# The end of an attention and gated-layer decode step: the result over 128 partitions, one 16-byte-run store, three rows of wo in eight-column products

## The chip, the cores and the metric

The kernel runs on one core of one Trainium2 chip. The metric is the device time of one launch in microseconds (us), of which the runs before the change gave 228.76 to 228.85, median 228.85. All times below are of this core. A core has a matrix engine (TensorE, in the profile PE, with its weight loads under PEld), VectorE (DVE), ScalarE (ACT), GpSimd (POOL), and SyncE (SP), which issues nearly all of this kernel's DMA. Products are summed in PSUM, everything else on the chip lies in SBUF, and both have 128 partitions.

## The reference, cut to what is computed

```python
x = A_x                                  # [2, 1, 512], two batches
xn = layernorm(x)
q = (xn @ wq) -> 32 heads of 128         # wq [512, 4096]
k, v = the last 4096 keys of the caches  # 8 key heads, each used by 4 query heads
o = softmax(q k^T / sqrt(128)) v         # [2, 32*128]
gate, up = xn @ W_gate, xn @ W_up        # [512, 1792]
h = gate * (gate > 0) * up
return x + o @ wo + h @ W_down           # wo [4096, 512], W_down [1792, 512]
```

Everything is f32. The output is two rows of 512 numbers, 4 KB; the inputs that are read are about 95 MB.

## The kernel before, in words

The inputs come in pieces of up to 4 MB through a ring of four SBUF buffers, all issued on SyncE's queue in the order of the program: `wq` in two pieces, `W_gate`, `W_up`, then for each of four groups of heads two pieces of `k` and two of `v`, then `W_down` (tile `dw`, in the profile `wd`), then `wo`. A piece is issued when its ring buffer has been read for the last time. The two halves of `x` come on ScalarE's queue.

Keys are transposed by VectorE (L257) and multiplied with the queries (L262); softmax, the products with the values (L325), a mask (L334) and a gather (L345) follow. The last group's results are spread over partitions in `spread_heads` (L363): TensorE makes tile `op`, and ScalarE copies it to `oT` (two columns a row of `wo`, one for each batch) and the last rows' part to `oT_rows`.

The end of the program is what the change is about. `o @ wo + h @ W_down + x` is a sum over 14 rows `k` of `W_down` and over 32 rows of `wo` (16 of `wo0`, 16 of `wo1`, index j), where a "row" holds 512 output columns for each of 128 partitions. There are two ways of adding one row:

- *Wide* (`project_wide`, L425): one product, two result rows (the batches) by 512 columns, into `yw_ps`. The n-th wide product goes to the strip of partitions that begins at 32 x (n mod 4), so that four strips of the array work at a time, each with partial sums of its own. ScalarE then copies `yw_ps` to `yw` (L459), and the *fold*, a product with a matrix of zeros and ones (`fold_rows`), adds the four strips.
- *Narrow* (`project`, L431): the 512 columns are cut in four quarters of 128, and each quarter's product goes to another strip of `y_ps`. The stationary operand has 17 columns, of which the first and the last are the batches and the rest zeros, so that the batches come to partitions 32e and 32e + 16. The fold and `x` go the same way.

Before the change 14 + 16 + 8 rows go wide and the last eight rows of `wo1` (`LAST`) go narrow. The first four of these come before the fold, j=12 to 14 and then j=15 (in two halves) after it. VectorE copies `y_ps` to `yo` (L467), and the store (L469) takes the 8 partitions that hold something, 2 runs of 64 numbers from each. `wo1` is loaded in pieces of 4, 4, 4, 2 and 1 rows (L448) and the last row in two halves (L454).

The order of the program is the order of each engine's queue (there is no scheduler). An instruction that waits holds up what stands behind it on its engine.

Of the kernel before, what the change touches and what calls it, by code (L numbers as in the profile page):

```python
# [9 lines left out]
F32 = mybir.dt.float32  # L10
# [10 lines left out]
def kernel(  # L21
# [12 lines left out]
    nc = tc.nc  # L34
    P = 128
    B, _, D = x.shape
# [5 lines left out]
    KC = D // P  # L42
# [3 lines left out]
    Q = 4  # L46
    C = 4
    R = HKV // C
# [6 lines left out]
    FB = F // P  # L55
# [19 lines left out]
    def load_wq(m):  # L75
        src = wq.rearrange("(p k) f -> p k f", p=P)[:, 2 * m:2 * m + 2, :]
        return load(f"wq{m}", src, [P, 2, HQ * DH])
# [17 lines left out]
    NJ = HQ * DH // (R * P)  # L95
# [3 lines left out]
    def wo_rows(r, j0, j1):  # L99
        rows = NJ * P  # L100
        return wo[r * rows:(r + 1) * rows, :].rearrange("(p j) e -> p j e", p=P)[:, j0:j1, :]


    x2 = const.tile([B, D], F32, name="x2")
    for half in (slice(0, D // 2), slice(D // 2, D)):
        nc.scalar.dma_start(x2[:, half], x[:, 0, half])
    wqt = [load_wq(m) for m in range(2)]

    ident = const.tile([P, P], F32, name="ident")
# [24 lines left out]
        out=pick[:, 8:16], in_=ident.rearrange("p (q u k) -> p k q u", q=Q, u=4), op=ALU.add, axis=AX.XY  # L134
# [3 lines left out]
        out=own_u, in_=ident.rearrange("p (q u k) -> p u q k", q=Q, u=4), op=ALU.add, axis=AX.XY  # L138
    )
    fold = const.tile([P, 32], F32, name="fold")  # L140
    nc.vector.tensor_reduce(
        out=fold, in_=ident.rearrange("p (q i) -> p i q", q=Q), op=ALU.add, axis=AX.X
    )
    fold_rows = const.tile([P, B, 16], F32, name="fold_rows")
    nc.gpsimd.memset(fold_rows, 0.0)
    nc.gpsimd.tensor_copy(fold_rows[:, :, 0], fold[:, 0:B])
    LAST = 8
    oT_rows = const.tile([P, LAST, B, 16], F32, name="oT_rows")
    nc.gpsimd.memset(oT_rows, 0.0)

    def rows(t):
        return t.rearrange("p b s -> p (b s)")[:, 0:17]


    HK = 2 * REP
# [2 lines left out]
    for h in range(2):  # L158
        nc.vector.tensor_reduce(
            out=by_h[:, :, h], in_=ident[:, PK * h:PK * h + PK].rearrange("p (x t k) -> p t k x", t=NP, k=REP),  # L160
            op=ALU.add, axis=AX.X,
# [29 lines left out]
        )  # L191
    xnT = const.tile([P, KC, 32], F32, name="xnT")
    nc.vector.tensor_copy(xnT, xt_ps)
    spare = const.tile([P, KC, 32], F32, name="spare")
    nc.gpsimd.memset(spare[:, 0], 0.0)


# [1 line left out]
    for kc in range(KC):  # L199
        for r in range(R):  # L200
            for c in range(C):
# [3 lines left out]
                    start=(kc == 0), stop=(kc == KC - 1),  # L205
# [3 lines left out]
    for r in range(R):  # L209
# [150 lines left out]
    def spread_heads(r):  # L360
        op = ps_1.tile([P, NJ, B], F32, name=f"op{r}", tag="misc")
        for e in range(NE):
            nc.tensor.matmul(  # L363
                op, spread.rearrange("h k e -> h (k e)")[:, NE - 1 - e:NE - 1 - e + P],
                osb[r][:, :, e * NJ:(e + 1) * NJ].rearrange("h b j -> h j b"),
                start=(e == 0), stop=(e == NE - 1),
            )
        if r == R - 1:
            nc.scalar.copy(oT_rows[:, :, :, 0], op[:, NJ - LAST:NJ])
        nc.scalar.copy(oT[:, r], op)  # L370

    for a in range(NP):
# [3 lines left out]
    def join(g, a):  # L376
        mask(g, a)
        gather(g, a)
        if a:
            total(g)  # L380

    def close(g):
        finish(g)
        if g % B == B - 1:
            spread_heads(g // B)
# [19 lines left out]
    dw = load_down()  # L405


    HC = P // 2
    y_ps = ps_kt.tile([P, 2, HC], F32, name="y_ps", tag="kt")
    nc.vector.memset(y_ps, 0.0)  # L410

    def quarter(row, e):
        return row.rearrange("p (h e c) -> p h e c", h=2, e=Q)[:, :, e]

    for e in range(Q):
        nc.tensor.matmul(
            y_ps[32 * e:32 * e + 17], rows(fold_rows)[0:B], quarter(x2, e), start=True, stop=False,
        )

    yw_ps = ps_kt.tile([P, D], F32, name="yw_ps", tag="kt")  # L420
    nc.vector.memset(yw_ps, 0.0)
    wide = FB + R * NJ - LAST
    done = [0]

    def project_wide(lhsT, w):  # L425
        n = done[0]
        done[0] += 1
        c = n % Q
        nc.tensor.matmul(yw_ps[32 * c:32 * c + B, :], lhsT, w, start=(n < Q), stop=(n >= wide - Q))  # L429

    def project(lhsT, w, halves=slice(0, 2), stop=False):  # L431
        for e in range(Q):
            nc.tensor.matmul(  # L433
                y_ps[32 * e:32 * e + 17, halves], lhsT, quarter(w, e)[:, halves], start=False, stop=stop,
            )

    for a in range(NP):
        values(g, a, vin[a])
        join(g, a)
    finish(g)  # L440
    for k in range(FB):
        project_wide(hT[:, k, 0:B], dw[:, k])
    spread_heads(R - 1)
    wots = []
    for r, cuts in ((0, (0, NJ)), (1, (0, 4, 8, 12, 14, 15))):
        wt = ring.tile([P, NJ, D], F32, name=f"wo{r}", tag="ring")
        for j0, j1 in zip(cuts, cuts[1:]):
            nc.sync.dma_start(wt[:, j0:j1], wo_rows(r, j0, j1))  # L448
        wots.append(wt)
    halves = [slice(h, h + 1) for h in range(2)]  # L450
    last = wots[R - 1][:, NJ - 1]
    for h in range(2):
        o = slice(h * D // 2, (h + 1) * D // 2)
        nc.sync.dma_start(last[:, o], wo_rows(R - 1, NJ - 1, NJ)[:, 0, o])  # L454
    for r in range(R):
        for j in range(NJ - (LAST if r == R - 1 else 0)):
            project_wide(oT[:, r, j], wots[r][:, j])
    yw = work.tile([P, D], F32, name="yw", tag="on")
    nc.scalar.copy(yw, yw_ps)  # L459
    for j in range(NJ - LAST, NJ - 1):  # L460
        if j == NJ - LAST + 4:
            project(rows(fold_rows), yw)
        project(rows(oT_rows[:, j - NJ + LAST]), wots[R - 1][:, j])
    yo = work.tile([P, 2, HC], F32, name="yo", tag="yo", bufs=1)
    for h in range(2):
        project(rows(oT_rows[:, LAST - 1]), last, halves[h], stop=h == 1)
    nc.vector.tensor_copy(yo, y_ps)  # L467

    nc.sync.dma_start(  # L469
        bass.AP(tensor=out.tensor, offset=out.offset, ap=[[HC, Q], [D, B], [D // 2, 2], [1, HC]]), yo[0:P:16]  # L470
    )


# [26 lines left out]
```

## Time and profile before

| what | us |
|---|---|
| median of three runs | 228.85 |
| lowest and highest | 228.76, 228.85 |
| the profiled execution | 228.92 |
| its span, first to last instruction | 227.1 |
| TensorE busy / VectorE busy / ScalarE busy / GpSimd busy | 125.3 / 118.5 / 14.3 / 4.3 |
| mean clock granted to TensorE | 0.819 of full |

The span is what the trace covers; the rest of the profiled execution's time lies around it. Times in the quoted views are counted from the span's start. "PE yw_ps L429" is a matrix product into `yw_ps` that line 429 of the kernel issues. Each product of f32 operands shows as two records, each with a weight load. "out<-in 128\*2 128x512" gives the shapes of the two operands. The bracket at the end of a timeline row is how long the engine was idle ahead of it, and what ended that.

### The profile page before, as it was taken

The page shows a single profiled execution, that of the slowest core. Times are in us where ns is not written, and L with a number is a line of the kernel's source. Part 1 is how long each engine was busy: PE and PEld are TensorE (multiplying, and loading weights), DVE is VectorE, ACT ScalarE, POOL GpSimd, SP SyncE. Part 2 cuts the span into 40 slices and gives each one's busy share as a digit, 9 for nine tenths or more (in the row PEclk, how much of TensorE's full clock was granted, in tenths as well). Part 3 has the DMA queues.
Part 4 walks back from the last instruction along what each step waited for, and adds up shares of the span by engine and source line. Part 5 has one row for each costly group of instructions (what it writes and reads, how often), then busy time and mean ns, then how long its engine had stood idle before and what let it go on. Part 6 is the DMA issues. An engine that isn't in the chain of part 4 may idle for free.

```text
span 227.1 us, 2122 instructions
## 1 busy us (share of the span) xinstructions
PE 125.3 (55%) x888; PEld 36.9 (16%) x888; DVE 118.5 (52%) x160; ACT 14.3 (6%) x41; POOL 4.3 (2%) x15
## 2 busy tenths in 40 slices
PE   0194926503636005876605876606857644889494
PEld 0141211101001001211201311201411201224113
DVE  2400043219893499963599893599369286011000
ACT  2000122000000500000200000200000110000001
POOL 7000000000000000000000000000000000000000
PEclk9999788955796555796985996985996996799769
DMA  7999999998999999999999999999999999999991
GB/s 277 462 398 426 470 414 413 462 450 387 456 457 392 439 462 404 424 462 421 415 456 444 395 450 456 398 439 456 407 427 462 415 418 456 408 434 447 394 413 68
DMA packets 4212, 95.03 MB, mean 418 GB/s; under 512 B 488, under 2 KB 748, under 8 KB 1004
## 3 DMA queue, kind: packets, MB, share of 16 engines
q1 hardware_dynamic: 4196, 94.90, 97.3%
q8 instruction: 7, 0.11, 0.2%
q14 instruction: 1, 0.01, 0.0%
q10 hardware_dynamic: 8, 0.00, 0.0%
HBM read 94.90 MB, written 0.00 MB: 418 GB/s over the span
## 4 chain that ended last, share of the span: by engine, by line
DMA 60%; DVE 20%; PE 14%; issue 3%; ACT 1%; SPq 0%; DVEq 0%; ACTq 0%
DMA k<-in_A_k_cache_dram 38%; DVE kT L257 16%; DMA wo<-in_A_wo_dram 13%; DMA wq<-in_A_wq_dram 9%; PE yw_ps L429 4%; PE s L262 3%; PE o L325 3%; PE q_ps L203 2%; DVE pt L306 2%; PE y_ps L433 1%; DVE on L334 1%; ACT pz L294 1%; DVE m L274 1%; ACT L294 1%; DVE pT L300 1%
## 5 line engine op out<-in xcount | busy, mean ns | idle before, releaser
L257 DVE STREAM_TRANSPOSE kT<-k 128x4096 f32<-128x4096 f32 x16 | 70.6, 4429 | 12.1 <-DMA k<-in_A_k_cache_dram 12.0
L262 PE MATMUL s<-kT,qz 128*32 128x512 f32 x256 | 43.7, 810 | 60.0 <-DVE kT L257 60.0
L325 PE MATMUL o<-v,pt 128*32 128x512 f32 x256 | 31.3, 618 | 0.0
L262 PEld LDWEIGHTS s<-kT,qz 128*32 128x32 f32 x256 | 8.7, 129 | 88.3 <-issue 62.8
L306 DVE COPY pt<-pT 32x256 f32<-32x256 f32 x64 | 18.2, 284 | 1.0
L345 PE MATMUL oa<-on,pick 128*16 128x512 f32 x16 | 9.8, 700 | 6.9 <-DVE on L334 6.9
L225 DVE COPY qz<-qt 32x32 f32<-32x32 f32 x16 | 3.0, 188 | 20.1 <-ACT qz L225 20.1
L203 PE MATMUL q_ps<-wq,xnT 128*32 128x512 f32 x64 | 11.3, 869 | 3.4 <-DMA wq<-in_A_wq_dram 3.0
L334 DVE TENSOR_TENSOR on<-o,own_u 128x512 f32<-128x512 f32 x8 | 5.4, 672 | 11.8 <-PE o L325 11.7
L325 PEld LDWEIGHTS o<-v,pt 128*32 128x32 f32 x256 | 8.5, 113 | 17.6 <-issue 17.5
L294 ACT ACTIVATE pz<-s,nm 64x512 f32<-64x512 f32 x8 | 5.9, 738 | 80.7 <-DVE nm L288 80.5
L429 PE MATMUL yw_ps<-wo,oT 128*2 128x512 f32 x48 | 8.3, 861 | 3.2 <-DMA wo<-in_A_wo_dram 3.2
L467 DVE COPY yo<-y_ps 128x128 f32<-128x128 f32 x1 | 0.3, 292 | 17.8 <-PE y_ps L433 17.8
L300 DVE STREAM_TRANSPOSE pT<-pz 128x1024 f32<-128x1024 f32 x4 | 5.0, 1245 | 8.3 <-ACT pz L294 8.3
L274 DVE TENSOR_REDUCE m<-s 128x1 f32<-128x512 f32 x4 | 2.8, 692 | 12.1 <-PE s L262 12.1
L188 PE MATMUL xt_ps<-rep,xc 2*128 2x32 f32 x8 | 2.1, 418 | 10.7 <-DVE rep L186 10.7
L233 PE MATMUL u_ps<-wu,xnT 128*32 128x448 f32 x32 | 3.2, 542 | 2.8 <-DMA wu<-in_B_W_up_dram 2.8
L203 PEld LDWEIGHTS q_ps<-wq,xnT 128*32 128x32 f32 x64 | 2.5, 154 | 11.4 <-issue 6.9
L233 PE MATMUL g_ps<-wg,xnT 128*32 128x448 f32 x32 | 4.2, 681 | 0.0
L214 PE MATMUL qt<-ident,qs 128*128 128x128 f32 x8 | 1.7, 354 | 4.4 <-DVE qs L211 4.4
L363 PEld LDWEIGHTS op<-osb,spread 16*128 16x128 f32 x32 | 3.7, 186 | 1.8 <-issue 1.8
L363 PE MATMUL op<-osb,spread 16*128 16x32 f32 x32 | 3.9, 273 | 0.0
(73 smaller groups left out, 53.2 us busy)
## 6 DMA issues: line engine op xcount, KB each, us to landing
k<-in_A_k_cache_dram SPq DMA_DIRECT2D x8, 4096.0 KB, 24.7
v<-in_A_v_cache_dram SPq DMA_DIRECT2D x8, 4096.0 KB, 27.7
wq<-in_A_wq_dram SPq DMA_DIRECT2D x2, 4096.0 KB, 16.7
wo<-in_A_wo_dram SPq DMA_DIRECT2D x1, 4096.0 KB
wg<-in_B_W_gate_dram SPq DMA_DIRECT2D x1, 3584.0 KB, 29.3
wu<-in_B_W_up_dram SPq DMA_DIRECT2D x1, 3584.0 KB, 38.3
wd<-in_B_W_down_dram SPq DMA_DIRECT2D x1, 3584.0 KB, 28.0
wo<-in_A_wo_dram SPq DMA_DIRECT2D x3, 1024.0 KB, 20.2
```

The lines of the kernel that those rows point to most:

```text
L203: nc.tensor.matmul(q_ps[r][32 * c:32 * c + 32, :], xnT[:, kc, :], wqt[kc // 2][:, kc % 2, n * 512:(n + 1) * 512], start=(kc == 0), stop=(k ...
L233: nc.tensor.matmul(dst[32 * c:32 * c + 32, :], xnT[:, kc, :], wt[:, kc, c * FQ:(c + 1) * FQ], start=(kc == 0), stop=(kc == KC - 1),)
L257: nc.vector.transpose(kt.rearrange("p j m i -> p j (m i)"), src)
L262: nc.tensor.matmul(ss[g][32 * q:32 * q + 32, :], qz[:, g, 2 * mh + m, a, h], kt[:, JS * s1:JS * s1 + JS, m, h::2], start=(a == 0 and mh == ...
L294: nc.scalar.activation(pv[o, :, :, h], ss[g][o].rearrange("p (j i) -> p j i", j=JS), AF.Exp, bias=nm[o], scale=SCALE, accum_out=l[o],)
L300: nc.vector.transpose(pT.rearrange("p j x t k -> p (j x t k)"), pz.rearrange("p j s -> p (j s)"))
L306: nc.vector.tensor_copy(pts[g][32 * x:32 * x + 32, :, s1, :, h], pT[q:q + 32, :, x].rearrange("p j t k -> p t j k"))
L325: nc.tensor.matmul(o[32 * q:32 * q + 32, :], pts[g][:, a, s1, j:j + 4].rearrange("p u h k -> p (u h k)"), v[:, lo:lo + 512], start=(s1 == ...
L334: nc.vector.tensor_tensor(ons[a], o.rearrange("p (u d) -> p u d", u=4), own_u[:, :, None].to_broadcast([P, 4, P]), op=ALU.mult)
L345: nc.tensor.matmul(oa[g].rearrange("h u d -> h (u d)"), pick[:, 8 - 8 * a:24 - 8 * a], ons[a].rearrange("p u d -> p (u d)"), start=(a == 0 ...
L363: nc.tensor.matmul(op, spread.rearrange("h k e -> h (k e)")[:, NE - 1 - e:NE - 1 - e + P], osb[r][:, :, e * NJ:(e + 1) * NJ].rearrange("h ...
L429: nc.tensor.matmul(yw_ps[32 * c:32 * c + B, :], lhsT, w, start=(n < Q), stop=(n >= wide - Q))
```

## The change

The result is laid out anew. `y_ps` is 128 x 32 and holds, in strip e, on partition 32e + 4b + k, the columns 128e + 4i + k of batch b for i from 0 to 31. VectorE turns each block of 32 x 32 (`transpose` for `tensor_copy`), after which partition p holds the columns 4p to 4p + 3 of both batches, and the store writes 2 x 4 numbers from each of 128 partitions. For that a narrow row is cut in four quarters and in each of these into four combs of every fourth column (`runs`): 16 products of 8 result rows by 32 columns. The stationary operand is an 8-column window of a 12-column strip with the batches at columns 3 and 7, moved by one for each comb.

Only three rows go narrow (`LAST = 3`, j=13 to 15), with the fold ahead of j=15. The rows j=8 to 12 go wide. `x` is added by a wide product with the identity in place of four narrow ones. `wo1` comes in pieces of 4, 4, 5, 1, 1 and 1 rows, and `x` in three pieces instead of two. The tile `spare` grows, which keeps the buffers behind it at their addresses.

```diff
-    for half in (slice(0, D // 2), slice(D // 2, D)):
-        nc.scalar.dma_start(x2[:, half], x[:, 0, half])
+    for lo, hi in ((0, P), (P, 2 * P), (2 * P, D)):
+        nc.scalar.dma_start(x2[:, lo:hi], x[:, 0, lo:hi])
...
-    fold_rows = const.tile([P, B, 16], F32, name="fold_rows")
+    RUN = 4
+    LAST = 3
+    fold_rows = const.tile([P, 3, RUN], F32, name="fold_rows")
-    LAST = 8
-    oT_rows = const.tile([P, LAST, B, 16], F32, name="oT_rows")
+    oT_rows = const.tile([P, LAST, 3, RUN], F32, name="oT_rows")
...
-    for e in range(Q):
-        nc.tensor.matmul(
-            y_ps[32 * e:32 * e + 17], rows(fold_rows)[0:B], quarter(x2, e), start=True, stop=False,
-        )
-    wide = FB + R * NJ - LAST
+    wide = 1 + FB + R * NJ - LAST
...
-    def project(lhsT, w, halves=slice(0, 2), stop=False):
-        for e in range(Q):
-            nc.tensor.matmul(
-                y_ps[32 * e:32 * e + 17, halves], lhsT, quarter(w, e)[:, halves], start=False, stop=stop,
-            )
+    def project(strip, row, start=False, stop=False):
+        runs = row.rearrange("p (e i k) -> p e k i", e=Q, k=RUN)
+        for k in range(RUN):
+            lhsT = strip.rearrange("p b k -> p (b k)")[:, RUN - 1 - k:3 * RUN - 1 - k]
+            for e in range(Q):
+                nc.tensor.matmul(
+                    y_ps[32 * e:32 * e + B * RUN], lhsT, runs[:, e, k],
+                    start=start and k == 0, stop=stop and k == RUN - 1,
+                )
+    project_wide(ident[0:B, 0:B], x2)
...
-    for r, cuts in ((0, (0, NJ)), (1, (0, 4, 8, 12, 14, 15))):
+    for r, cuts in ((0, (0, NJ)), (1, (0, 4, 8, 13, 14, 15, 16))):
...
-    for j in range(NJ - LAST, NJ - 1):
-        if j == NJ - LAST + 4:
-            project(rows(fold_rows), yw)
-        project(rows(oT_rows[:, j - NJ + LAST]), wots[R - 1][:, j])
-    yo = work.tile([P, 2, HC], F32, name="yo", tag="yo", bufs=1)
-    for h in range(2):
-        project(rows(oT_rows[:, LAST - 1]), last, halves[h], stop=h == 1)
-    nc.vector.tensor_copy(yo, y_ps)
+    for j in range(NJ - LAST, NJ):
+        if j == NJ - 1:
+            project(fold_rows, yw)
+        project(oT_rows[:, j - NJ + LAST], wots[R - 1][:, j], start=j == NJ - LAST, stop=j == NJ - 1)
+    yo = work.tile([P, 32], F32, name="yo", tag="yo", bufs=1)
+    nc.vector.transpose(yo, y_ps)
     nc.sync.dma_start(
-        bass.AP(tensor=out.tensor, offset=out.offset, ap=[[HC, Q], [D, B], [D // 2, 2], [1, HC]]), yo[0:P:16]
+        bass.AP(tensor=out.tensor, offset=out.offset, ap=[[RUN, P], [D, B], [1, RUN]]),
+        yo[:, 0:B * RUN].rearrange("p (b k) -> p b k", b=B),
     )
```

TensorE's queue from the products with `wd` to the end of the program, before the change (a row is a line, a product, its operands and shape, and how many of it follow one another; `op` is the spreading of the heads, the first `wo` tile is `wo0`, the second `wo1`):

```order
L429 MATMUL yw_ps<-wd,hT 2x512 x14
L363 MATMUL op_830<-osb_748,spread 128x32 x8
L429 MATMUL yw_ps<-wo_841,oT 2x512 x16
L429 MATMUL yw_ps<-wo_843,oT 2x512 x8
L433 MATMUL y_ps<-wo_843,oT_rows 17x128 x16
L433 MATMUL y_ps<-yw,fold_rows 17x128 x4
L433 MATMUL y_ps<-wo_843,oT_rows 17x128 x12
L433 MATMUL y_ps<-wo_843,oT_rows 17x64 x8
```

The same stretch of TensorE's queue after the change:

```order
L418 MATMUL yw_ps<-wd,hT 2x512 x14
L361 MATMUL op_828<-osb_749,spread 128x32 x8
L418 MATMUL yw_ps<-wo_839,oT 2x512 x16
L418 MATMUL yw_ps<-wo_841,oT 2x512 x13
L425 MATMUL y_ps<-wo_841,oT_rows 8x32 x32
L425 MATMUL y_ps<-yw,fold_rows 8x32 x16
L425 MATMUL y_ps<-wo_841,oT_rows 8x32 x16
```

Five rows have moved from the narrow products to the wide ones, ahead of `yw`'s copy, and two narrow rows instead of four stand ahead of the fold, one instead of four behind it. A narrow row is 16 products where it was four.

SyncE's queue from the load of `wd` to the end, before the change (line, transfer, its shape):

```order
L71 DMA wd<-in_B_W_down_dram 128x7168
L448 DMA wo_841<-in_A_wo_dram 128x8192
L448 DMA wo_843<-in_A_wo_dram 128x2048 x3
L448 DMA wo_843<-in_A_wo_dram 128x1024
L448 DMA wo_843<-in_A_wo_dram 128x512
L454 DMA wo_843<-in_A_wo_dram 128x256 x2
L469 DMA out_dram<-yo 4x4x64
```

And after it:

```order
L71 DMA wd<-in_B_W_down_dram 128x7168
L442 DMA wo_839<-in_A_wo_dram 128x8192
L442 DMA wo_841<-in_A_wo_dram 128x2048 x2
L442 DMA wo_841<-in_A_wo_dram 128x2560
L442 DMA wo_841<-in_A_wo_dram 128x512 x3
L456 DMA out_dram<-yo 128x2x4
```

The third piece of `wo1` has five rows instead of four, the last row comes whole, and the store goes from 4 x 4 runs of 64 numbers to 128 x 2 runs of four.

More of the change, by code (lines that the diff above doesn't have):

```diff
@@ L143 @@
     )
-    fold_rows = const.tile([P, B, 16], F32, name="fold_rows")
+    RUN = 4
+    LAST = 3
+    fold_rows = const.tile([P, 3, RUN], F32, name="fold_rows")
     nc.gpsimd.memset(fold_rows, 0.0)
-    nc.gpsimd.tensor_copy(fold_rows[:, :, 0], fold[:, 0:B])
-    LAST = 8
-    oT_rows = const.tile([P, LAST, B, 16], F32, name="oT_rows")
+    nc.gpsimd.tensor_copy(fold_rows[:, 0:B, RUN - 1], fold[:, 0:B])
+    oT_rows = const.tile([P, LAST, 3, RUN], F32, name="oT_rows")
     nc.gpsimd.memset(oT_rows, 0.0)
-    def rows(t):
-        return t.rearrange("p b s -> p (b s)")[:, 0:17]
     HK = 2 * REP
@@ L193 @@
     nc.vector.tensor_copy(xnT, xt_ps)
-    spare = const.tile([P, KC, 32], F32, name="spare")
+    spare = const.tile([P, KC, 90], F32, name="spare")
     nc.gpsimd.memset(spare[:, 0], 0.0)
@@ L368, in spread_heads @@
         if r == R - 1:
-            nc.scalar.copy(oT_rows[:, :, :, 0], op[:, NJ - LAST:NJ])
+            nc.scalar.copy(oT_rows[:, :, 0:B, RUN - 1], op[:, NJ - LAST:NJ])
         nc.scalar.copy(oT[:, r], op)
@@ L405 @@
     dw = load_down()
-    HC = P // 2
-    y_ps = ps_kt.tile([P, 2, HC], F32, name="y_ps", tag="kt")
+    y_ps = ps_kt.tile([P, 32], F32, name="y_ps", tag="kt")
     nc.vector.memset(y_ps, 0.0)
-    def quarter(row, e):
-        return row.rearrange("p (h e c) -> p h e c", h=2, e=Q)[:, :, e]
-    for e in range(Q):
-        nc.tensor.matmul(
-            y_ps[32 * e:32 * e + 17], rows(fold_rows)[0:B], quarter(x2, e), start=True, stop=False,
-        )
     yw_ps = ps_kt.tile([P, D], F32, name="yw_ps", tag="kt")
     nc.vector.memset(yw_ps, 0.0)
-    wide = FB + R * NJ - LAST
+    wide = 1 + FB + R * NJ - LAST
     done = [0]
@@ L449 @@
         wots.append(wt)
-    halves = [slice(h, h + 1) for h in range(2)]
-    last = wots[R - 1][:, NJ - 1]
-    for h in range(2):
-        o = slice(h * D // 2, (h + 1) * D // 2)
-        nc.sync.dma_start(last[:, o], wo_rows(R - 1, NJ - 1, NJ)[:, 0, o])
     for r in range(R):
@@ L459 @@
     nc.scalar.copy(yw, yw_ps)
-    for j in range(NJ - LAST, NJ - 1):
-        if j == NJ - LAST + 4:
-            project(rows(fold_rows), yw)
-        project(rows(oT_rows[:, j - NJ + LAST]), wots[R - 1][:, j])
-    yo = work.tile([P, 2, HC], F32, name="yo", tag="yo", bufs=1)
-    for h in range(2):
-        project(rows(oT_rows[:, LAST - 1]), last, halves[h], stop=h == 1)
-    nc.vector.tensor_copy(yo, y_ps)
+    for j in range(NJ - LAST, NJ):
[4 more added lines that the diff above has]
+    nc.vector.transpose(yo, y_ps)
     nc.sync.dma_start(
-        bass.AP(tensor=out.tensor, offset=out.offset, ap=[[HC, Q], [D, B], [D // 2, 2], [1, HC]]), yo[0:P:16]
+        bass.AP(tensor=out.tensor, offset=out.offset, ap=[[RUN, P], [D, B], [1, RUN]]),
+        yo[:, 0:B * RUN].rearrange("p (b k) -> p b k", b=B),
     )
```

## The prediction

> **What bounds the kernel now.** I began with the page: how long the span is, and whether one resource fills it. The last line is the busy share of the DMA engines in 40 slices.
>
> ```profile
> span 227.1 us, 2122 instructions
> PE 125.3 (55%) x888; PEld 36.9 (16%) x888; DVE 118.5 (52%) x160; ACT 14.3 (6%) x41; POOL 4.3 (2%) x15
> DMA  7999999998999999999999999999999999999991
> ```
>
> No engine is over 55%, and DMA is full in every slice but the first and the last. So the stream of inputs sets the time up to the end, and the change moves no byte of it: what it can win or lose lies behind the last input bytes, and in their order. Next I read the chain that ended last, from the wait for `wo` on (start, length, what).
>
> ```profile
> 184.09 29.75 DMA wo<-in_A_wo_dram
> 213.84 0.04 issue
> 213.89 8.28 PE yw_ps L429 x48
> 222.17 2.05 PE y_ps L433 x80
> ```
>
> From 213.89 on nothing on the chain waits for DMA: TensorE itself is the end. The timeline shows how it goes through its work. The columns are start, length, instruction, count, and in brackets the idle time before it.
>
> ```profile
> 207.30 0.13 PEld L429 LDWEIGHTS yw_ps<-wd,hT 128*2 128x2 f32 x2 [0.30 <-issue]
> 207.73 0.13 PEld L429 LDWEIGHTS yw_ps<-wd,hT 128*2 128x2 f32 x2 [0.30 <-issue]
> ...
> 213.89 8.28 PE L429 MATMUL yw_ps<-wo,oT 128*2 128x512 f32 x48 [3.20 <-DMA wo<-in_A_wo_dram]
> ...
> 219.82 0.13 PEld L429 LDWEIGHTS yw_ps<-wo,oT 128*2 128x2 f32 x4 [0.71 <-issue]
> 220.28 0.10 PEld L429 LDWEIGHTS yw_ps<-wo,oT 128*2 128x2 f32 x4 [0.33 <-issue]
> ...
> 221.57 0.11 PEld L433 LDWEIGHTS y_ps<-wo,oT_rows 128*17 128x17 f32 x4 [0.34 <-issue]
> 222.00 1.05 PE L433 MATMUL y_ps<-wo,oT_rows 128*17 128x128 f32 x32
> ...
> 222.25 0.59 ACT L459 COPY yw<-yw_ps 128x512 f32<-128x512 f32 x1 [11.20 <-PE yw_ps L429]
> 222.88 0.41 PE L433 MATMUL y_ps<-yw,fold_rows 128*17 128x128 f32 x8
> ...
> 223.11 1.06 PE L433 MATMUL y_ps<-wo,oT_rows 128*17 128x128 f32 x40
> 224.24 0.29 DVE L467 COPY yo<-y_ps 128x128 f32<-128x128 f32 x1 [17.80 <-PE y_ps L433]
> 224.56 0.68 SPq L469 DMA_DIRECT2D out_dram<-yo  x1
> ```
>
> Each f32 product leaves two records (48 for 24 wide rows), so it is done in two passes. Wide rows go four at a time, one in each strip of 32 columns of the array, and a step of four records takes 0.84 us up to 219.82 (0.71 + 0.13) and 0.43 us after 220.28 (0.33 + 0.10; three steps to 221.57). The first two rows above matter most: 14 rows of `wd` leave two over, and these two take two steps of 0.43 us (207.73 and one more before the next weights) although half of the strips are empty. **A started round of four costs as much as a full one.** So 24 rows are 6 rounds, 12 steps, the last of which starts at 221.57. A narrow row takes 0.66/3 = 0.22 us: three of them, j=12 to 14, fill 223.11 to 223.77 at two passes of four products each.
>
> **Part by part.** (1) *Five more wide rows.* In the changed kernel `yw_ps` takes 16 + 13 = 29 rows of `wo` where it took 24. 29 rows are 8 rounds, 16 steps: four more, at 0.43 us, **+1.72 us** before ScalarE's copy of `yw`, where 5/4 of a round would be 1.07 us. Is the pace 0.43 there, and are the rows there in time? The stretches below are us, then the busy time of each engine, the clock granted to TensorE, and DMA.
>
> ```profile
> 209.63:213.05 3.42, 1.06 (x10) 0.95 (x9) 0.00 (x0) 0.26 (x2) 0.00 (x0) 1.00 0.86 369
> 213.05:216.46 3.41, 2.57 (x16) 0.46 (x20) 0.00 (x0) 0.00 (x0) 0.00 (x0) 0.50 1.00 423
> 216.46:219.87 3.41, 3.41 (x24) 0.58 (x20) 0.00 (x0) 0.00 (x0) 0.00 (x0) 0.50 0.99 418
> 219.87:223.29 3.42, 3.42 (x72) 1.63 (x68) 0.00 (x0) 0.59 (x1) 0.00 (x0) 1.00 0.74 286
> ```
>
> The clock is halved after the idle stretch before 213.05 and whole from 219.87, so the added steps run whole. The three landings below are those of j=4 to 7 (issued at 198.6), j=12 and 13 (199.6) and the last half row (204.2).
>
> ```profile
> L448 SPq DMA_DIRECT2D wo<-in_A_wo_dram x1: 428/428/428, 198.6 to 198.6; - x1
> ...
> DMA to landing us min/median/max: 20.2/20.2/20.2
> L448 SPq DMA_DIRECT2D wo<-in_A_wo_dram x1: 432/432/432, 199.6 to 199.6; - x1
> ...
> DMA to landing us min/median/max: 22.9/22.9/22.9
> L454 SPq DMA_DIRECT2D wo<-in_A_wo_dram x1: 328/328/328, 204.2 to 204.2; - x1
> ...
> DMA to landing us min/median/max: 19.6/19.6/19.6
> ```
>
> That is 218.8, 222.5 and 223.8 us. Six rows in 3.7 us make 0.61 us a row, so the new piece j=8 to 12 lands near 218.8 + 5 x 0.61 = 221.8 us, and its first row is due after 12 steps, at 222.00. DMA and TensorE stand within 0.2 us of each other. So were the clock whole earlier, the data would still hold the end: four steps from 221.9 give the last start at 223.2, against 222.00 + 3 x 0.43 = 223.3. Term (1) lies between +1.6 and +1.72; I take 1.72.
>
> (2) *Three narrow rows leave the end.* Behind the fold of `yw` stood j=12 to 15; now only j=15 does, and j=13 and 14 lie under the copy. That is **-0.66 us** (three at 0.22). The last row lands near 223.8, before the fold can begin (222.88 + 1.72 = 224.6), so DMA has no part in it.
>
> (3) *A row in 16 products of 32 columns instead of four of 128.* The columns streamed are the same. At 0.109 us for 128 columns (0.22/2) a step of 32 is 0.027, and the fold and the last row, 16 such steps, take the 0.44 us they took before. The nearest measured step is that of the 64-column halves: ten steps fill the 1.06 us from 223.11 less the 0.22 us of the last product, six of them take 0.66, and four share the rest, 0.05 each. If 32 columns go no faster than 64, 16 steps take 0.8, so **0** to +0.4; I take 0, since cost follows the columns from 512 (0.43) over 128 (0.109) to 64.
>
> (4) *A VectorE transpose of 128x32 for a copy of 128x128.* No transpose is this small.
>
> ```profile
> 180.50 0.16 DVE L288 COPY nm<-nm_ps 128x1 f32<-128x1 f32 x1 [0.53 <-PE nm_ps L286]
> L257 DVE STREAM_TRANSPOSE kT<-k x4: 4401/4424/4446, 50.1 to 64.3; 128x4096 f32<-128x4096 f32 x4
> L300 DVE STREAM_TRANSPOSE pT<-pz x4: 1245/1245/1246, 77.2 to 182.4; 128x1024 f32<-128x1024 f32 x4
> L243 DVE STREAM_TRANSPOSE hT<-hh x1: 939/939/939, 44.4 to 44.4; 128x448 f32<-128x448 f32 x1
> ```
>
> From 1024 to 4096 columns it is 3.18/3072 = 1.04 ns a column, which leaves 0.18 us for none and about 0.21 for 32, against 0.29 now: **-0.08 us**. The ends are a one-column copy out of PSUM, 0.16, and the 448-column transpose with its split rows, 0.94: -0.13 to +0.65.
>
> (5) *The store.* The first row is its issue, the second that of the `wo` pieces over 128 partitions. The last three are the stretches from its issue's end to the landing that SyncE sees.
>
> ```profile
> L469 SPq DMA_DIRECT2D out_dram<-yo x1: 684/684/684, 224.6 to 224.6; - x1
> L448 SPq DMA_DIRECT2D wo<-in_A_wo_dram x6: 327/428/432, 184.1 to 200.0; - x6
> 225.25:225.84 0.59, 0.00 (x0) 0.00 (x0) 0.00 (x0) 0.00 (x0) 0.00 (x0) 1.00 0.00 0
> 225.84:225.97 0.13, 0.00 (x0) 0.00 (x0) 0.00 (x0) 0.00 (x0) 0.00 (x0) 1.00 0.15 32
> 225.97:226.31 0.34, 0.00 (x0) 0.00 (x0) 0.00 (x0) 0.00 (x0) 0.00 (x0) 1.00 0.00 0
> ```
>
> Issue 0.68, nothing 0.59, bytes 0.13, receipt 0.34. Over 128 partitions the issue should cost 0.33 to 0.43, a gain of 0.25 to 0.36. The bytes go in 256 pieces of 16 B where 16 of 256 B went in 0.13 us: from no change to 16 times that. They come from 128 partitions instead of 8, so I take +0.1 and keep +0.5 for the range: **-0.2 us**, from -0.36 to +0.25. The Trainium skill ("DMA: Bandwidth & Descriptors", "Why a DMA increments its semaphore by 16 and not by 1") says that a transfer uses the largest number of engines up to 16 that divides the slowest dimensions, and that the sequencer writes the missing increments itself. By that the store goes from 4 engines to 16 and 12 such writes go; the long issue of 0.684 agrees, and the sum stays.
>
> (6) *What is covered.* The product of `x` becomes two passes of 512 columns behind the `yw_ps` memset, at half clock about 1.7 us ahead of the `values` products. The 3.20 us in which TensorE waits for `wo` before 213.89 hide it; without them it would cost up to 1.7. A third piece of `x`, one more issue on ScalarE's queue, is late by less than the 3.0 us below, and one fewer `wo` issue on SyncE's queue falls 20 us before its landing.
>
> ```profile
> 22.47 1.08 PE L203 MATMUL q_ps<-wq,xnT 128*32 128x512 f32 x4 [3.04 <-DMA wq<-in_A_wq_dram]
> ```
>
> Sum: 1.72 - 0.66 + 0 - 0.08 - 0.2 = +0.78 us. The profiled execution took 228.92 us, its span and 1.8 around it, and becomes 229.7; the runs shown have a median 0.07 lower, 228.85, so **229.6 us**.
>
> **Rivals.** *Small products cost by the piece.* For it: the 40 records in the 1.06 us from 223.11 could be read as 26 ns each, whatever their width. Then the 64 records of the fold and the last row would take 64 x 26 = 1.7 us where I have 0.44: +1.2, 230.8 us. Against it: 24 of the 40 lie in the 0.66 us of three 128-column rows, 27 ns each, and the other 16 in the last 0.2 us of starts, 12 ns each, so cost follows columns. The Trainium skill ("TensorE: Matmul & The Clock Gate", "Wait — 56ns, not 53.3ns?") states such a floor, about 25 ns from one start to the next however few the columns. The 12 ns speak against it where four strips take turns, and so I give it a small chance only.
>
> *The store shrinks more, and the change is not slower.* Place: from the issue at 224.56 to 226.31, 1.75 us. If the spread over 128 partitions cut the 1.06 us behind the issue by half as well, the store saves 0.53 + 0.3 and the sum is +0.15: 229.0. From 0.5 us saved it is within 0.2%; from about 1.5 saved, faster. Against it: the 0.59 and 0.34 us hold no bytes, so a wider spread should not shorten them.
>
> *TensorE waits warm and cools.* If the delayed `values` products keep the clock whole at 213.05, TensorE runs out of rows near 219.5, idles 2.4 us, and may be halved again at 223.29: the fold, the last row and the last pass at half clock, +0.6, 230.2. Against it: the wait before 213.05 stays 1.5 us.
>
> *16-byte pieces are slow to land*, the upper end of (5): +0.45, 230.1.
>
> **How the numbers follow.** Forecast 0.62; piece cost 0.12; short store 0.13; cooling 0.06; slow pieces 0.07. A measurement of this kernel can tell about 0.2%, 0.46 us, from no change. Slower holds all but the short store and the forecast's low edge: 0.80; same 0.14; faster 0.06. The range reaches down to 229.0, the short store's time, and up to 230.7, past the two small rivals and most of the piece cost.
>
> **What would show it.** Right: 58 records of `wo` in `yw_ps` in 16 steps, two records in the last two; ScalarE's copy near 224.0; the fold near 224.6 and 0.45 us to the last product; issue below 0.45. Wrong: a step that holds the 29th row beside narrow products so that the copy starts before 223.5, steps of over 0.05 us in the narrow rows, a transpose over 0.3, or `wo` landing elsewhere than at 213.8 and 223.8.

## The result, and the profile after

The changed kernel takes 230.2 us (median of six runs, 230.14 to 230.64) against 228.83 (six runs, 228.76 to 229.01): a ratio of 1.0062, with a 95% interval of 1.0049 to 1.0075. It is slower by 1.37 us. The prediction was 229.6 us with a range of 229.0 to 230.7: the sign and the range hold, and the forecast of +0.78 us is 0.59 us short.

The page of the changed kernel, with its length, its busy times and its DMA shares:

```profile
span 228.4 us, 2225 instructions
PE 128.3 (56%) x940; PEld 37.5 (16%) x940; DVE 118.4 (52%) x160; ACT 14.3 (6%) x41; POOL 4.1 (2%) x15
DMA  7999999999899999989999998999999999999990
```

The span has grown by 1.3 us, nearly all of the difference. DMA is as full as before, so the place to look is again the end. The chain that ended last there:

```profile
200.88 20.97 DMA wo<-in_A_wo_dram
221.89 1.08 PE yw_ps L418 x9
222.98 0.19 PE y_ps L425 x11
223.18 0.59 PE yw_ps L418
223.77 1.95 PE y_ps L425 x106
225.74 0.22 DVE yo L454
```

Before, the chain left DMA at 213.84 and TensorE worked alone from there. Now it leaves DMA at 221.89: the piece with five rows, j=8 to 12, holds TensorE up. The timeline of the same stretch (start, length, instruction, count, idle time before it):

```profile
213.99 7.03 PE L418 MATMUL yw_ps<-wo,oT 128*2 128x512 f32 x48 [2.37 <-DMA wo<-in_A_wo_dram]
...
221.89 1.45 PE L418 MATMUL yw_ps<-wo,oT 128*2 128x512 f32 x9 [0.87 <-DMA wo<-in_A_wo_dram]
...
222.76 0.41 PE L425 MATMUL y_ps<-wo,oT_rows 128*8 128x32 f32 x12
...
223.18 0.59 PE L418 MATMUL yw_ps<-wo,oT 128*2 128x512 f32 x1
...
223.81 0.59 ACT L448 COPY yw<-yw_ps 128x512 f32<-128x512 f32 x1 [11.84 <-PE yw_ps L418]
224.45 0.28 PE L425 MATMUL y_ps<-yw,fold_rows 128*8 128x32 f32 x5
...
224.98 0.73 PE L425 MATMUL y_ps<-wo,oT_rows 128*8 128x32 f32 x28
225.74 0.22 DVE L454 STREAM_TRANSPOSE yo<-y_ps 128x32 f32<-128x32 f32 x1 [17.50 <-PE y_ps L425]
225.98 0.40 SPq L456 DMA_DIRECT2D out_dram<-yo  x1
```

The added rounds start at 221.89, four steps from there end in the copy at 223.81, and the fold starts at 224.45. From the fold's first product to VectorE it is now 1.29 us (225.74 - 224.45) for a fold and one row, where it was 1.36 us (224.24 - 222.88) for a fold and four rows. From the fold's start to the row of the last 28 records (224.98) it is 0.53 us, in which 36 records start, nine steps of four strips: about 60 ns for 32 columns.

The rows below are stretches of the span: us, busy time of PE, PEld, DVE, ACT and POOL, the clock granted to TensorE, DMA share, GB/s. The first four are the stream's end, the last four the store, from its issue to the landing that SyncE sees.

```profile
211.80:215.21 3.41, 1.22 (x12) 0.32 (x16) 0.00 (x0) 0.17 (x2) 0.00 (x0) 1.00 0.98 413
215.21:218.62 3.41, 3.41 (x20) 0.68 (x16) 0.00 (x0) 0.00 (x0) 0.00 (x0) 0.50 1.01 428
218.62:222.04 3.42, 2.55 (x28) 0.53 (x24) 0.00 (x0) 0.00 (x0) 0.00 (x0) 1.00 0.96 389
222.04:225.45 3.41, 3.41 (x137) 2.37 (x130) 0.00 (x0) 0.59 (x1) 0.00 (x0) 1.00 0.16 61
225.98:226.39 0.41, 0.00 (x0) 0.00 (x0) 0.00 (x0) 0.00 (x0) 0.00 (x0) 1.00 0.00 0
226.39:226.90 0.51, 0.00 (x0) 0.00 (x0) 0.00 (x0) 0.00 (x0) 0.00 (x0) 1.00 0.00 0
226.90:227.15 0.25, 0.00 (x0) 0.00 (x0) 0.00 (x0) 0.00 (x0) 0.00 (x0) 1.00 0.59 17
227.15:227.58 0.43, 0.00 (x0) 0.00 (x0) 0.00 (x0) 0.00 (x0) 0.00 (x0) 1.00 0.00 0
```

The clock is whole in every one of these stretches from 218.62 on. The store takes 0.41 + 0.51 + 0.25 + 0.43 = 1.60 us, where it took 0.68 + 0.59 + 0.13 + 0.34 = 1.75 (225.25 - 224.56 for the first).

The differences add up: the fold starts 1.57 later; from there to VectorE 0.07 less; VectorE 0.08 less (0.29 to 0.22); the store 0.15 less. That is +1.27 us beside a span that grew by 1.3.

### The profile page after: what moved, and what is told of

Its sections match the earlier page's. It is cut to its first block, busy times and chain, and to the rows that moved or that the text cites. A ratio compares the mean times of both kernels' runs of the same rounds, so it can differ in the third digit from the quotient of the medians.

```text
span 228.4 us, 2225 instructions
## 1 busy us (share of the span) xinstructions
PE 128.3 (56%) x940; PEld 37.5 (16%) x940; DVE 118.4 (52%) x160; ACT 14.3 (6%) x41; POOL 4.1 (2%) x15
## 4 chain that ended last, share of the span: by engine, by line
DMA 57%; DVE 24%; PE 12%; issue 3%; ACT 2%; SPq 0%; DVEq 0%; ACTq 0%
DMA k<-in_A_k_cache_dram 39%; DVE kT L255 15%; DMA wq<-in_A_wq_dram 9%; DMA wo<-in_A_wo_dram 9%; DVE pt L304 4%; PE o L323 4%; PE s L260 3%; PE q_ps L201 2%; PE yw_ps L418 2%; ACT pz L292 1%; DVE on L332 1%; DVE pT L298 1%; PE y_ps L425 1%; PE oa L343 1%; DVE m L272 1%
## 5 line engine op out<-in xcount | busy, mean ns | idle before, releaser
L323 PE MATMUL o<-v,pt 128*32 128x512 f32 x256 | 33.4, 654 | 0.0
L323 PEld LDWEIGHTS o<-v,pt 128*32 128x32 f32 x256 | 9.0, 118 | 20.4 <-issue 20.3
L418 PE MATMUL yw_ps<-wo,oT 128*2 128x512 f32 x58 | 8.9, 721 | 3.2 <-DMA wo<-in_A_wo_dram 3.2
L201 PE MATMUL q_ps<-wq,xnT 128*32 128x512 f32 x64 | 9.8, 764 | 1.1 <-DMA wq<-in_A_wq_dram 0.7
L231 PE MATMUL u_ps<-wu,xnT 128*32 128x448 f32 x32 | 4.9, 776 | 4.2 <-DMA wu<-in_B_W_up_dram 4.2
L240 DVE TENSOR_TENSOR hh<-gs,u_ps 128x448 f32<-128x448 f32 x1 | 0.6, 621 | 7.9 <-PE u_ps L231 7.9
L186 PEld LDWEIGHTS xt_ps<-rep,xc 2*128 2x128 f32 x8 | 1.9, 322 | 13.2 <-DVE rep L184 13.2
```

Of the source, the lines that this page charges most:

```text
L201: nc.tensor.matmul(q_ps[r][32 * c:32 * c + 32, :], xnT[:, kc, :], wqt[kc // 2][:, kc % 2, n * 512:(n + 1) * 512], start=(kc == 0), stop=(k ...
L231: nc.tensor.matmul(dst[32 * c:32 * c + 32, :], xnT[:, kc, :], wt[:, kc, c * FQ:(c + 1) * FQ], start=(kc == 0), stop=(kc == KC - 1),)
L323: nc.tensor.matmul(o[32 * q:32 * q + 32, :], pts[g][:, a, s1, j:j + 4].rearrange("p u h k -> p (u h k)"), v[:, lo:lo + 512], start=(s1 == ...
```

## The experiments

All are read by their spans and by the same rows as above: the fold's start, VectorE's start, the store. Their times are compared with runs of the kernel before on the same chips (medians 228.81 to 228.91, spans near 227.1). Where a run changes the size of other tiles, `spare` is resized with them to keep the load buffers in their place, except where it is said. The theory ahead of the first three: a step of a narrow row costs 60 ns because each comb takes one f32 number out of every 16 bytes. The rivals: all four combs are added to the same 32 addresses of PSUM and wait for each other; a small product has a floor of 60 ns.

### Neighbouring columns instead of combs

```diff
-        runs = row.rearrange("p (e i k) -> p e k i", e=Q, k=RUN)
+        runs = row.rearrange("p (e k i) -> p e k i", e=Q, k=RUN)
```

> The four combs of a quarter become four blocks of 32 neighbouring columns, so the result's columns land in other places. In the changed kernel a strip takes 60 ns from one 32-column pass to the next. If reading every fourth number costs (stride), a step falls to about 30 ns, and the 16 steps of the fold and the last row take 0.5 us instead of 0.96: about 0.5 us off the changed kernel, 229.7 us. If a pass has a floor of its own (floor), or if sums into the same PSUM columns must be 60 ns apart (same address), the step stays at 60 ns and the time at 230.2.

The timeline at the end:

```profile
224.37 0.42 PE L425 MATMUL y_ps<-yw,fold_rows 128*8 128x32 f32 x32
...
224.61 0.48 PE L425 MATMUL y_ps<-wo,oT_rows 128*8 128x32 f32 x32
225.15 0.22 DVE L454 STREAM_TRANSPOSE yo<-y_ps 128x32 f32<-128x32 f32 x1 [15.27 <-PE y_ps L425]
```

The eight steps of the fold take 0.24 us, 30 ns each, and from the fold to VectorE it is 0.78 us: 0.51 less than with combs. Only the stride of the streamed operand differs. The span falls to 227.8 to 228.1. The time does not follow: 230.19 us (229.7 to 230.28), ratio 1.0060 (1.0045 to 1.0074), as with combs (230.20, 1.0062). Three of the four runs lie 2.2 to 2.4 us over their span; the section on the prediction comes back to this. So the cost of the stride is shown inside the span, and not in the time of the launch.

### Each comb at its own place in PSUM

```diff
-    y_ps = ps_kt.tile([P, 32], F32, name="y_ps", tag="kt")
+    y_ps = ps_kt.tile([P, RUN, 32], F32, name="y_ps", tag="kt")
...
-                    y_ps[32 * e:32 * e + B * RUN], lhsT, runs[:, e, k],
+                    y_ps[32 * e:32 * e + B * RUN, k], lhsT, runs[:, e, k],
...
-    nc.vector.transpose(yo, y_ps)
+    nc.vector.transpose(yo, y_ps[:, RUN - 1])
```

> Each of the four combs sums into 32 columns of PSUM of its own, and only the fourth block is turned and stored. Same address: the step falls from 60 to about 30 ns except between the two passes of one product, 16 steps in about 0.6 us. Floor and stride: 60 ns as before, 0.96 us.

The span of its one run was 228.3 us and the time 230.57. The end in the timeline:

```profile
224.41 0.23 PE L425 MATMUL y_ps<-yw,fold_rows 128*8 128x32 f32 x3
...
224.94 0.71 PE L425 MATMUL y_ps<-wo,oT_rows 128*8 128x32 f32 x28
225.69 0.22 DVE L454 STREAM_TRANSPOSE yo<-y_ps 128x32 f32<-128x32 f32 x1 [16.59 <-PE y_ps L425]
```

With no address shared between combs the same 28 records take 0.71 us, beside 0.73, and from the fold to VectorE it is 1.28 us, beside 1.29. The addresses in PSUM are not the cause.

### Half of each comb

```diff
-                    y_ps[32 * e:32 * e + B * RUN], lhsT, runs[:, e, k],
+                    y_ps[32 * e:32 * e + B * RUN, 0:16], lhsT, runs[:, e, k, 0:16],
```

> Only the first 16 of the 32 columns of each comb are multiplied; the others are left out. Floor: the step stays at 60 ns though half of the columns are gone. Stride (a cost for each column, 1.9 ns): the step falls to about 30 ns. Same address: stays at 60 ns.

The span of its one run was 227.9 us and the time 229.76. The end in the timeline:

```profile
224.45 0.43 PE L425 MATMUL y_ps<-yw,fold_rows 128*8 128x16 f32 x32
...
224.70 0.46 PE L425 MATMUL y_ps<-wo,oT_rows 128*8 128x16 f32 x32
```

Eight steps in 0.25 us, 31 ns each for 16 columns: 1.9 ns a column as with 32 (60/32), so there is no floor at 60 ns. Neighbouring columns take 0.94 ns (30/32).

The Trainium skill states a rule that fits ("SBUF — State Buffer", "Door 1: The DMA port swizzle"): SBUF is read in lines of 16 bytes, and an access pattern needs at least two hits in each line for full bandwidth. A comb of every fourth f32 number has one hit in each line. The rate of these three runs agrees; what goes on inside the memory none of them shows.

### The row split alone, in the layout of before

The output's layout stays as before the change, with combs, transpose and store undone; three rows go narrow, the pieces are cut at 13, and the fold stands ahead of j=15.

```diff
-    LAST = 8
+    LAST = 3
...
-    for r, cuts in ((0, (0, NJ)), (1, (0, 4, 8, 12, 14, 15))):
+    for r, cuts in ((0, (0, NJ)), (1, (0, 4, 8, 13, 14, 15))):
...
     for j in range(NJ - LAST, NJ - 1):
-        if j == NJ - LAST + 4:
-            project(rows(fold_rows), yw)
         project(rows(oT_rows[:, j - NJ + LAST]), wots[R - 1][:, j])
+    project(rows(fold_rows), yw)
```

> The kernel before with only the rows split as in the change: 29 rows of wo wide, j=13 to 15 narrow in products of 128 columns, the old layout, copy and store. If the eighth round of wide products and the five-row piece of wo delay the fold by 1.56 us as in the changed kernel's trace, and three narrow rows of 0.22 us leave the end, it is 0.9 us over the kernel before: 229.7, with the fold near 224.45. If the whole loss lies in the small products and the layout, it stays at 228.8.

The timeline at the end:

```profile
222.09 1.45 PE L429 MATMUL yw_ps<-wo,oT 128*2 128x512 f32 x9 [0.88 <-DMA wo<-in_A_wo_dram]
...
224.00 0.59 ACT L459 COPY yw<-yw_ps 128x512 f32<-128x512 f32 x1 [12.17 <-PE yw_ps L429]
224.64 0.41 PE L433 MATMUL y_ps<-yw,fold_rows 128*17 128x128 f32 x8 [0.24 <-ACT yw L459]
...
225.35 0.29 DVE L466 COPY yo<-y_ps 128x128 f32<-128x128 f32 x1 [18.11 <-PE y_ps L433]
```

Spans of 227.9 to 228.2, so +1.0 us comes from the row split alone. The fold starts at 224.64, 0.19 later than expected, because the products that wait for the piece of five rows start at 222.09 here and at 221.89 in the changed kernel. From the fold to VectorE it is 0.71 us, where the prediction had 1.36 - 0.66 = 0.70: its term (2) is met to 0.01 when the products stay dense. The time was 230.08 us (229.76 to 231.19), ratio 1.0064 (1.0047 to 1.0081), 0.4 over the expected 229.7. So in the time the split alone makes 1.27 us (230.08 beside 228.81) of the change's 1.37, in the span 1.0 of 1.3.

### One wide row fewer, and a cut at j=12

Twenty-eight rows of `wo` are seven full rounds; the second kernel keeps 29 and only cuts the piece of five.

```diff
-    LAST = 3
+    LAST = 4
...
-    for r, cuts in ((0, (0, NJ)), (1, (0, 4, 8, 13, 14, 15, 16))):
+    for r, cuts in ((0, (0, NJ)), (1, (0, 4, 8, 12, 14, 15, 16))):
```

> The changed kernel with 28 rows of wo wide instead of 29 (LAST = 4, j=12 narrow, wo1 in pieces of 4, 4, 4, 2, 1, 1). Rounds: 28 rows are seven rounds of four, the last wide step starts near 221.7 instead of 223.2, and TensorE then has 3 narrow rows, the fold and the last row at 0.48 us each from the landing of j=12 near 222.5: the last product starts near 224.9 instead of 225.47, 0.6 us off the changed kernel's span, 227.8. If a wide row costs its quarter of a round (0.21 us) and a narrow one 0.48, one row moved back costs 0.27 us: span 228.6.

```diff
-    for r, cuts in ((0, (0, NJ)), (1, (0, 4, 8, 13, 14, 15, 16))):
+    for r, cuts in ((0, (0, NJ)), (1, (0, 4, 8, 12, 13, 14, 15, 16))):
```

> The changed kernel with the five-row piece of wo1 cut into four rows and one, nothing else. If the landing of the five-row piece (221.85) holds the eight wide rounds, j=8 to 11 begin near 221.3 and j=12 near 222.2, and the fold, which then waits for the two narrow rows ahead of it, starts near 224.0 instead of 224.45: 0.4 us off the span, 227.9. If TensorE's own pace holds them, nothing changes: 228.3.

The timeline with 28 wide rows:

```profile
221.76 0.10 PEld L418 LDWEIGHTS yw_ps<-wo,oT 128*2 128x2 f32 x4 [0.33 <-issue]
...
222.62 1.61 PE L425 MATMUL y_ps<-wo,oT_rows 128*8 128x32 f32 x96
...
222.87 0.59 ACT L448 COPY yw<-yw_ps 128x512 f32<-128x512 f32 x1 [10.45 <-PE yw_ps L418]
...
224.04 0.68 PE L425 MATMUL y_ps<-yw,fold_rows 128*8 128x32 f32 x32
```

And with the cut at 12:

```profile
221.30 1.88 PE L418 MATMUL yw_ps<-wo,oT 128*2 128x512 f32 x10 [0.20 <-DMA wo<-in_A_wo_dram]
...
223.21 0.59 ACT L448 COPY yw<-yw_ps 128x512 f32<-128x512 f32 x1 [9.93 <-PE yw_ps L418]
```

Without the 29th row the copy starts 0.94 us earlier (223.81 to 222.87). This run also has the piece of five rows cut, but here TensorE did not wait for it: the last full round starts at 221.76 (the first row above), beside 221.89 in the changed kernel. So 0.13 us at most come from the earlier piece, and the rest is about the two steps of 0.43 us that the 29th row opened. The fold gains only 0.41, because three narrow rows of 60 ns steps now stand between (222.62 to 224.04). With the cut alone the copy starts 0.60 earlier (223.81 to 223.21), because the last full round starts at 221.30: the landing of the piece of five rows, not TensorE, held the last rounds. Spans were 227.8 to 228.3 and 227.7 to 228.2; times 230.29 us (230.13 to 230.55), ratio 1.0060 (1.0048 to 1.0073), and 230.03 us (229.77 to 230.6), ratio 1.0052 (1.0039 to 1.0065).

### Two combs of 64 columns, one number in every 8 bytes

The store then needs runs of two numbers (8 bytes), in two transfers on two queues.

```diff
-    RUN = 4
+    RUN = 2
...
-        runs = row.rearrange("p (e i k) -> p e k i", e=Q, k=RUN)
+        runs = row.rearrange("p (m e i k) -> p e k m i", m=2, e=Q, k=RUN)
...
+    for m, queue in enumerate((nc.sync, nc.scalar)):
+        queue.dma_start(
+            bass.AP(tensor=out.tensor, offset=out.offset + m * (D // 2), ap=[[RUN, P], [D, B], [1, RUN]]),
+            yo[:, m, 0:B * RUN].rearrange("p (b k) -> p b k", b=B),
+        )
```

> The changed kernel with two combs of 64 columns (every second number, 8 bytes apart) instead of four of 32 (every fourth, 16 bytes apart). The result is stored in two halves, on SyncE's and ScalarE's queues, 2 numbers a run. If only the 16-byte stride halves the reading, a step of 64 columns takes 0.056 us, the fold and the last row 0.45 instead of 0.96 us, and with 0.1 us more for the store the span is 0.4 us shorter, 227.9. If any stride costs 1.9 ns a column, a step takes 0.12 us, and nothing is won: 228.4.

A second kernel adds before's split of the rows (`LAST = 8`, before's cuts, the fold after j=11):

> The new layout with two combs of 64 columns as in the run before, and the rows split as in the kernel before: 24 wide, eight narrow, the fold after j=11, pieces of 4, 4, 4, 2, 1, 1. If the loss is the eighth round, the five-row piece and the 16-byte stride, and nothing else, TensorE ends within 0.2 us of the kernel before, the transpose takes 0.05 us less than the copy and the store 0.1 less: the span is that of before, 227.0 to 227.2, so the same time, 228.8. If the layout costs something else, it stays above 227.5.

The first missed both of its cases and the second the one that named a time; it is above 227.5, as its last case says. The spans were 229.4 to 229.6 and 229.6 to 229.9 us, the times 231.73 us (231.52 to 231.86), ratio 1.0125 (1.0109 to 1.0140), and 231.75 us (231.51 to 231.81), ratio 1.0122 (1.0108 to 1.0136). The first one's timeline, and then two of its stretches, the store's bytes and what follows them up to the landing:

```profile
224.38 0.41 PE L425 MATMUL y_ps<-yw,fold_rows 128*4 128x64 f32 x16 [0.22 <-ACT yw L448]
...
225.09 0.25 DVE L454 STREAM_TRANSPOSE yo<-y_ps 128x64 f32<-128x64 f32 x1 [15.45 <-PE y_ps L425]
```

```profile
226.20:226.76 0.56, 0.00 (x0) 0.00 (x0) 0.00 (x0) 0.00 (x0) 0.00 (x0) 1.00 0.48 8
226.76:228.47 1.71, 0.00 (x0) 0.00 (x0) 0.00 (x0) 0.00 (x0) 0.00 (x0) 0.80 0.00 0
```

TensorE did what was expected: 0.71 us from fold to VectorE, as with dense products. The store did not: 1.71 us from the last byte to the landing, where 16-byte runs took 0.43. Is it the runs or the two queues? The changed kernel with its store in two, one batch on each queue, in 16-byte runs:

```diff
+    for b, queue in enumerate((nc.sync, nc.scalar)):
+        queue.dma_start(
+            bass.AP(tensor=out.tensor, offset=out.offset + b * D, ap=[[RUN, P], [1, RUN]]),
+            yo[:, b * RUN:(b + 1) * RUN],
+        )
```

> The changed kernel with its store in two, one for each batch, on SyncE's and ScalarE's queues, in runs of 16 bytes as before. In e7_two_combs two stores in runs of 8 bytes landed 1.7 us after their last bytes had moved. If the two queues did that, it is so here too, and the span near 229.9. If the 8-byte runs did it, the landing comes about 0.45 us after the last bytes and the span stays at 228.4.

Its last two stretches, from the last byte to the landing on SyncE's queue:

```profile
227.02:227.20 0.18, 0.00 (x0) 0.00 (x0) 0.00 (x0) 0.00 (x0) 0.00 (x0) 1.00 0.00 0
227.20:227.61 0.41, 0.00 (x0) 0.00 (x0) 0.00 (x0) 0.00 (x0) 0.00 (x0) 1.00 0.00 0
```

The one run took 230.42 us with a span of 228.6, 0.2 to 0.3 over the changed kernel's, and landed 0.59 us after its last byte. So two queues cost 0.16 of the 1.28 us between 1.71 and 0.43. What is left are the runs: they are 8 bytes long, and there are 512 of them in place of 256. These two were not separated.

In the second kernel the inputs came later as well: its last `wo` row landed at 224.93, not 223.74. One thing that differed was the size of `spare`, which put the ring of load buffers 32 bytes off. The changed kernel with nothing but that:

```diff
-    spare = const.tile([P, KC, 90], F32, name="spare")
+    spare = const.tile([P, KC, 88], F32, name="spare")
```

> The changed kernel with spare two columns smaller, which moves the ring's buffers by 32 bytes, as happened unmeant in e8_two_combs_24_wide, where every 4 MB piece took 9.72 us instead of 9.66. If the place of the buffers makes the stream slower, the last row of wo lands near 224.9 instead of 223.74 and the span is 229.5. If not, 223.7 and 228.4.

Its timeline, where the last four wide steps begin:

```profile
223.00 1.45 PE L418 MATMUL yw_ps<-wo,oT 128*2 128x512 f32 x9 [1.14 <-DMA wo<-in_A_wo_dram]
```

Its one run took 231.35 us with a span of 229.5, and what waits for the piece of five rows starts at 223.00 instead of 221.89. In this run a shift of 32 bytes cost 1.1 us. So the change's own enlargement of `spare` matters, and both kernels that are compared have their buffers at the same, better place.

### Pairs: two neighbours in every 16 bytes, with before's split of the rows

This puts together what the runs had shown to cost nothing (24 wide rows, the transpose, the store in 16-byte runs) and one thing not yet tried: pairs of neighbours in place of single numbers.

```diff
-    RUN = 4
-    LAST = 3
+    RUN = 2
+    LAST = 8
...
-        runs = row.rearrange("p (e i k) -> p e k i", e=Q, k=RUN)
+        runs = row.rearrange("p (e i k t) -> p e k i t", e=Q, k=RUN, t=2)
...
-                    y_ps[32 * e:32 * e + B * RUN], lhsT, runs[:, e, k],
+                    y_ps[32 * e:32 * e + B * RUN].rearrange("p t i -> p i t"), lhsT, runs[:, e, k],
...
-    for r, cuts in ((0, (0, NJ)), (1, (0, 4, 8, 13, 14, 15, 16))):
+    for r, cuts in ((0, (0, NJ)), (1, (0, 4, 8, 12, 14, 15, 16))):
...
-        if j == NJ - 1:
+        if j == NJ - LAST + 4:
...
-    nc.vector.transpose(yo, y_ps)
+    nc.vector.transpose(yo.rearrange("p q t -> p t q"), y_ps)
```

> What the runs before leave as the best of both: 24 rows wide and eight narrow as in the kernel before; a narrow row in two combs of 64 columns each, read in neighbouring pairs (two numbers every 16 bytes); the result turned into runs of 16 bytes and stored in one DMA over 128 partitions as in the change. If pairs are read at the full rate, a step takes 0.056 us, TensorE ends near 224.2 as before the change, the transpose of 128x64 takes 0.25, the store 1.6 us: span 227.0, within 0.2 us of the kernel before, so nothing that can be told from it. If every step of 16 bytes halves the rate, a step takes 0.12 us and the last row ends 0.3 us later: span 227.3.

The timeline at the end:

```profile
222.31 0.59 ACT L448 COPY yw<-yw_ps 128x512 f32<-128x512 f32 x1 [9.62 <-PE yw_ps L418]
...
222.98 0.42 PE L425 MATMUL y_ps<-yw,fold_rows 128*4 128x64 f32 x16
...
223.21 1.12 PE L425 MATMUL y_ps<-wo,oT_rows 128*4 128x64 f32 x64
224.41 0.25 DVE L454 STREAM_TRANSPOSE yo<-y_ps 128x64 f32<-128x64 f32 x1 [15.46 <-PE y_ps L425]
224.69 0.40 SPq L456 DMA_DIRECT2D out_dram<-yo  x1
```

The four steps of the fold take 0.23 us, 58 ns for 64 columns, the dense rate. The copy is back at 222.31. The time is 228.82 us (median of 11, 228.77 to 229.42) beside 228.91 (15 runs, 228.7 to 229.17): a ratio of 0.9999 (0.9990 to 1.0008). That is 1.4 us better than the changed kernel and no different from the one before. VectorE starts at 224.41, 0.17 later than before the change (224.24), which uses up what the transpose and the store gain. No kernel tried here is faster than the one before.

## Why the prediction was right in sign and half of the size

- **(1) Five more wide rows, +1.72.** Measured +1.57 at the fold's start, just under the lower bound of +1.6. The mechanism is the one written: whole rounds of four, and the piece with five rows landing when TensorE needs it (predicted 221.8; the products that wait for it start at 221.89). The 29th row alone in its round cost its two full steps (28 wide rows: 0.94 us earlier, of which 0.13 at most come from the cut piece). TensorE started `wo` at a whole clock, at 213.99, and was halved only in the stretch from 215.21, so it ran ahead and waited; the landing was the bound that held.
- **(2) Three narrow rows leave the end, -0.66.** Right: the row split alone gives 0.71 us from the fold to VectorE where 0.70 was due.
- **(3) Narrow products of 32 columns at no cost: the term that was mis-sized.** It measured +0.59 us (1.29 - 0.70) where 0 was taken and +0.4 was the upper bound. The step as the prediction put it, "cost follows the columns" down to 0.027 us, is right for neighbouring columns (30 ns) and wrong for every fourth one (60 ns). Sixteen such steps are 0.96 us instead of 0.44: +0.52 of the 0.59; the other 0.07 is also there with neighbouring columns (0.78 against 0.71). The nearest rows that the prediction used were all dense; the new operand differed from them in width and in stride, and only the width was bounded. One of the prediction's own signs of being wrong was a step of over 0.05 us in the narrow rows; the 0.06 us were it.
- **(4) Transpose, -0.08.** Right: 0.22 us for 0.29.
- **(5) Store, -0.2.** Right, -0.15: the issue 0.40, the bytes +0.12, the receipt 0.09 longer.
- **(6) Covered work.** Right: TensorE's wait for `wo` shrank from 3.20 to 2.37 us and the products of `wo` still started at 213.99, 0.1 later.

With +0.59 in (3), +1.57 in (1), -0.65 in (2) and -0.15 in (5), the prediction's own sum gives 1.57 - 0.65 + 0.59 - 0.08 - 0.15 = +1.28. That 230.2 still lies in the range is in part luck: the upper part of the range was kept for a cost by the piece and for slow pieces of the store, and the stride, which filled it, is named nowhere in the prediction.

**The rivals.** "Small products cost by the piece" gave 230.8 and came near in size, but falls as a mechanism: half the columns take half the time at the same count. The Trainium skill's floor of about 25 ns from start to start ("TensorE: Matmul & The Clock Gate", "Wait — 56ns, not 53.3ns?") does not show between strips: with four of them taking turns, 32 records in 0.25 us are 8 ns apart. Within one strip the steps are 30 ns apart, so a floor of 25 ns there is not excluded. The short store did not happen: the stretches without bytes stayed (0.51 and 0.43 us). TensorE did not cool at the end: its clock is whole from 218.62. The store in pieces of 16 bytes was not slow; the one in pieces of 8 bytes was.

**What stays open.** In the kernel before and the changed one nearly all runs lie 1.7 to 1.9 us over their spans; one of the kernel before lies 2.28 over, and the profiled run of the changed one 2.24. In most runs of the kernels with neighbouring columns, with 28 wide rows and with the cut at 12 it is 2.2 to 2.5, in two runs of the row split alone 2.9 and 3.3. What happens there lies behind the span, and only one thing is seen of it: in the seven of the thirteen profiled runs that lie 2.1 to 2.4 us over their spans, a transfer of 8 KB on a queue that the page calls `instruction` starts 1.7 to 2.1 us behind the span's end (at 230.5 in the changed kernel). The six others lie 1.8 to 1.9 over, and only one of them, the store in two, has it. Whether the transfer lengthens a run, or is seen because the run lasts longer, is not shown. So these kernels' times do not show the few tenths that their spans gained, and they are judged by their spans and timelines alone.

## What to carry to other kernels

When a streamed operand is cut into combs, bound its cost by stride as well as by width: take at least two f32 numbers out of every 16 bytes, as pairs and every second number did here at the dense rate. Before rows are moved into a stage that works in rounds, count the rounds that they open and the landing of the piece that carries them; here one row beyond a full round cost two steps of 0.43 us ahead of the copy, and the piece of five rows 0.6. A shorter end (fewer products, a cheaper store) is only a gain as far as the work moved ahead of it was covered there.

## What the hardware did that was not expected

- One f32 number out of every 16 bytes streams into TensorE at 1.9 ns a column, one out of every 8 bytes and two neighbours out of every 16 at 0.9.
- The same pairs were written to PSUM with neighbours 128 bytes apart, at no cost (58 ns for 64 columns). The Trainium skill ("SBUF — State Buffer", "Door 1: The DMA port swizzle") says that any pattern in PSUM that isn't contiguous slows products down a lot; this run doesn't show that.
- A store of 4 KB to HBM landed 1.71 us after its last byte in 512 runs of 8 bytes on two queues, 0.59 in 256 runs of 16 bytes on two queues, 0.43 in 256 runs of 16 bytes and 0.34 in 16 runs of 256 bytes on one.
- Load buffers shifted by 32 bytes made the whole stream later by 1.1 to 1.2 us at its end, in two kernels with one trace each. Why was not tried.
